# Pooled attention with a feed-forward layer: one block maximum as the bias of the exponential, half-height transposes, a ring of three banks for the maxima

## The chip, the cores and the metric

One core of one Trainium2 chip. The metric is the device time of one execution in microseconds: the median of the timed runs. TensorE is called PE, VectorE DVE, ScalarE ACT, GpSimd POOL, SyncE SP.

## The reference

Inputs q, k, v are 4 x 8 heads x 1152 x 64 in float32, drawn with a deviation of about 0.71 (0.1 x 7.123 and 0.1 x 7.13) for q and k. Queries are averaged two by two, so there are 576 per head.

```python
q_pool = q.reshape(B, H, S // 2, 2, D).mean(axis=3)
scores = 1.0 / np.sqrt(D) * np.matmul(q_pool, k.transpose(0, 1, 3, 2))
scores = scores - np.max(scores, axis=-1, keepdims=True)
attn = np.exp(scores)
attn = attn / (np.sum(attn, axis=-1, keepdims=True) + 1e-09)
attn_out = np.matmul(attn, v)                                  # (4, 8, 576, 64)
x = attn_out.transpose(0, 2, 1, 3).reshape(4 * 576, 512)
h = np.maximum(x @ w_in, 0.0)                                  # 512 -> 2048
out = (h * h) @ w_out                                          # 2048 -> 512
```

## The kernel before

`run` builds the whole computation twice: once with quick maxima, and once more (`exact`) behind a flag that is read at the end (a branch on `again`); with these inputs the second isn't executed. In it stand first the attention, then the feed-forward part.

**Attention.** Work goes by pairs of heads, 16 of them (`pairs`, index n). The two heads of a pair lie on partitions 0 to 63 and 64 to 127, so a matmul of one head uses half of the array's rows and the two heads' matmuls stand side by side (`rows(h)`). For a pair: `load_q`, `load_k`, `load_v` (DMAs from SP); `pool_q` adds neighbouring queries on POOL; `prep` (units u = 0 to 3) transposes keys and queries on PE into a PSUM bank; `prep_high` (ACT) writes the rounded high part and `prep_low` (DVE) the remainder, so that a product is made from three matmuls. `squares` (ACT) keeps sums for the flag.

`maxes` (12 units) computes quick scores with queries on the partitions, in two PSUM banks, one for each head; `max_left` reduces them on DVE to a negated maximum for each query row, `max_fin` joins the parts, `max_turn` transposes the result on PE and `max_rows` copies it on ACT into `MM`, a row of negated maxima for each query.

The queries are then taken in two halves (e = 0, 1) of 288. `scores` makes for each of 9 chunks of 128 keys a tile of keys x queries of both heads: four terms of two matmuls, the three products and a matmul of ones with `MM`, which subtracts each query's maximum. `expo` (ACT) writes the exponential into a buffer `p` (three buffers in all, each for a run of 4 or 5 chunks, `CYCLE`). `pv` multiplies with the values on PE (stationary values of 64 columns for each head, so the array is used in another shape). `add` sums the exponentials of the nine chunks on POOL with four instructions in a half (L375); `total` sums over the partitions on PE; `total_x` (ACT) copies, `recip` (DVE) inverts in two pieces, `pv_x` (ACT) brings out the values' result and `scale_x` (POOL, L398) multiplies.

**PSUM.** 8 banks: score tiles 2 x 2 banks (`sps`), maxima 2 (`mps`, one tile for both heads), 1 for transposes and totals (`tps`, handed out by `bank`), 1 for values (`vps`).

**The order** is written out by hand: `at(key, name, fn, ..., after=...)` gives each step a key, raised to just behind the keys of the steps named in `after`; all steps are sorted by key and issued in that order, and each engine works through its own steps in that order. The numbers in `AT` shift the steps' keys. A pair has 4 units of key (`NCY`); pair n's scores start at key 4 n.

In the last pair (n = 15) the weights of the feed-forward part are converted on DVE between the other steps (`convert`, key -0.8 to 3.4 after the pair's start; L111 to L125, POOL joins with L127).

**Feed-forward.** Five passes over 5 blocks of tokens; `layer1` and `layer2` with three matmuls for each product; `out_rows` gives for a tile of 128 tokens the rows of the output and `layer2` sends them, alternating between the queues of SP and ACT.

Of the kernel before, what the change touches and what calls it, by code (L numbers as in the profile page):

```python
# [21 lines left out]
    e=-0.666, h0=-1.798, h1=-0.099, h2=0.09, h3=-0.731, l0=-2.259, l1=-1.892, l2=-1.181, l3=-2.391, m0=3.23,  # L22
    mr0=-0.125, mr1=0.928, pq=-0.619, px=1.044, r0=-0.773, r1=-3.214, r10=-0.653, r11=-2.477, r2=0.853, r3=0.12,
    r4=-1.46, r5=-1.28, r6=-0.268, r7=-0.491, r8=-0.663, r9=-0.675, rc00=0.606, rc01=0.974, rc10=-2.759,
    rc11=-1.537, sq0=2.106, sq1=-0.737, sq2=2.477, sx=-0.655, t0=1.92, t1=2.58, tx=0.115, u0=-3.77, u1=0.23,
    u2=0.55, u3=1.23, x0=1.22, x1=1.3, x10=4.46, x11=2.14, x2=-1.95, x3=2.22, x4=2.46, x5=1.53, x6=3.05, x7=3.22,
    x8=3.53, x9=4.14,
# [3 lines left out]
EXACT = 8192.0  # L31


@with_exitstack
def kernel(
# [31 lines left out]
    def run(ctx, exact):  # L67
# [89 lines left out]
        with ExitStack() as a:  # L157
# [6 lines left out]
            mps = a.enter_context(tc.tile_pool(name="mps", bufs=1, space=PSUM))  # L164
            tps = a.enter_context(tc.tile_pool(name="tps", bufs=1, space=PSUM))
# [5 lines left out]
            QQ = [[kq.tile([P, NQ], F32R, name=f"qq{i}{m}") for m in range(2)] for i in range(2)]  # L171
# [5 lines left out]
            NM = [kq.tile([P, 2, 64], F32, name=f"nm{i}") for i in range(2)]  # L177
            MM = [[kq.tile([P, NH], F32R, name=f"mm{i}{m}") for m in range(2)] for i in range(2)]
            MASK = kq.tile([P, NT5], F32, name="mask")
            ONER = kq.tile([P, P], F32R, name="oner")  # L180
# [4 lines left out]
            SQ = kq.tile([P, 3, NP], F32, name="sq")  # L185
            ld_, qp_, b_, s_, m_, p_, t_, pv_, r_ = ({} for _ in range(9))
# [24 lines left out]
            def pool_q(n):  # L211
                qt, ql = ld_.pop(("q", n))
                qp = ld.tile([P, NR, 2, D], F32, tag="qp", name="qp")
                qpl = ld.tile([NL, 2, D], F32, tag="qpl", name="qpl")
                nc.gpsimd.tensor_tensor(out=qp.rearrange("p r h d -> p h r d"), in0=qt[:, :, :, 0, :],
                                        in1=qt[:, :, :, 1, :], op=ALU.add)
                nc.gpsimd.tensor_tensor(out=qpl, in0=ql[:, :, 0, :], in1=ql[:, :, 1, :], op=ALU.add)
                qp_[n] = qp, qpl


            def squares(n, e):
                x = [ld_["k", n], *qp_[n]][e]
# [272 lines left out]
            for x in NM:  # L495
                nc.vector.memset(x, 0.0)
# [161 lines left out]
```

## Time and profile before

| | |
|---|---|
| timed runs | 916.15, 916.32, 917.96 us; median 916.32 |
| profiled execution, span from first to last instruction | 914.7 us |
| busy: PE / DVE / POOL / ACT | 874.5 / 651.7 / 481.0 / 449.4 us |
| score matmuls (L332), the three products | 1728 |
| score matmuls (L332), with ones | 576 |
| maxima L303, reductions of 128 x 1024 | 160 |
| output DMAs | 28 (8 of 256 KB, 20 of 128 KB) |

The profile holds one execution. Its own time outside the span isn't recorded; the median of the timed runs lies 1.6 us above the span. Engines run beside each other; a long busy time is no bound by itself, and matmuls are pipelined, so that their shown durations overlap. Durations of one instruction are means in ns where a group is shown, and the start and length in us where single instructions are shown.

### The profile page before, as it was taken

Reading aid. Unit: us, or ns where it says so; the run is one execution under the profiler, and the core shown is the slowest. Engines: PE = TensorE matmul, PEld = TensorE weight load, DVE = VectorE, ACT = ScalarE, POOL = GpSimd, SP = SyncE. Lnnn points to the kernel's source line nnn. Section 1 sums busy time; section 2 is a strip of 40 time slices with the busy share of each in tenths; the row PEclk is TensorE's granted clock in tenths of the full one; section 3 lists DMA queues with packets and bytes.
Section 4 is the critical chain, followed back from the end, with each engine's and each line's share of the span. In section 5 each row is a group of like instructions: output and inputs, shape, how many; then the busy total and the mean of one; then the engine's idle time right before and its main releaser. Section 6 shows DMA issues by size and latency. Waiting matters only on the chain.

```text
span 914.7 us, 15275 instructions
## 1 busy us (share of the span) xinstructions
PE 874.5 (96%) x6182; PEld 649.2 (71%) x6182; DVE 651.7 (71%) x849; ACT 449.4 (49%) x876; POOL 481.0 (53%) x261
## 2 busy tenths in 40 slices
PE   6999999999999999999968989999999999999996
PEld 4666666666666666666635868778888888888885
DVE  5667667676776767776799998988877676655543
ACT  2665665666656566665625546333342433333321
POOL 1488988898888988889786342431320311110000
PEclk9999999999999999999979999999999999999999
DMA  7122222122221222230011121211210101000213
GB/s 206 27 64 65 56 73 59 56 60 70 54 78 52 54 78 53 79 98 2 27 47 47 47 70 47 69 51 42 59 51 30 47 24 47 24 1 1 70 47 95
DMA packets 61968, 50.88 MB, mean 56 GB/s; under 512 B 39104, under 2 KB 49344, under 8 KB 61888
## 3 DMA queue, kind: packets, MB, share of 16 engines
q1 hardware_dynamic: 61088, 48.50, 18.5%
q10 hardware_dynamic: 800, 1.31, 0.4%
q8 instruction: 50, 0.82, 0.4%
q14 instruction: 30, 0.25, 0.1%
HBM read 45.09 MB, written 4.72 MB: 54 GB/s over the span
## 4 chain that ended last, share of the span: by engine, by line
PE 79%; DVE 11%; issue 3%; ACT 3%; POOL 2%; DMA 1%; SPq 0%; ACTq 0%; DVEq 0%; POOLq 0%
PE o L580 17%; PE h L543 17%; PE s L332 16%; PE pv L349 16%; PE m L291 7%; DVE pm L303 4%; PE t L243 2%; PE t L385 2%; POOL r L127 1%; DVE a L116 1%; DVE xlo L150 1%; ACT p L342 1%; PE t L249 1%; DVE h L119 1%; PE t L314 1%
## 5 line engine op out<-in xcount | busy, mean ns | idle before, releaser
L303 DVE TENSOR_REDUCE pm<-m 128x2 f32<-128x1024 f32 x154 | 188.5, 1224 | 58.1 <-PE m L291 58.0
L342 ACT ACTIVATE p<-s 128x576 f32<-128x576 f32 x288 | 176.9, 650 | 67.6 <-PE s L332 63.3
L375 POOL TENSOR_TENSOR ts<-p 128x2304 f32<-128x2304 f32 (+1 forms) x32 | 157.4, 4918 | 58.8 <-ACT p L342 58.8
L332 PE MATMUL s<-qq,kk 64*128 64x288 f32 x1728 | 174.5, 311 | 1.9 <-ACT p L342 1.2
L543 PE MATMUL h<-xhi,wi 128*128 128x512 f32 (+1 forms) x600 | 171.1, 370 | 3.4 <-ACT wi L137 3.4
L580 PE MATMUL o<-wo,gh 128*128 128x512 f32 x540 | 167.3, 391 | 2.5 <-DVE part L588 2.4
L349 PE MATMUL pv<-p,vt 128*64 128x288 f32 x1152 | 158.5, 416 | 0.0
L127 POOL TENSOR_TENSOR r<-r,h 128x512 f32<-128x512 f32 x32 | 51.4, 1607 | 202.3 <-DVE r L125 193.3
L332 PEld LDWEIGHTS s<-qq,kk 64*128 64x128 f32 x1728 | 129.5, 186 | 34.2 <-issue 19.6
L543 PEld LDWEIGHTS h<-xhi,wi 128*128 128x128 f32 x600 | 110.6, 190 | 23.7 <-ACT wi L137 3.6
L375 POOL TENSOR_TENSOR ts<-ts 128x1152 f32<-128x1152 f32 (+1 forms) x60 | 121.6, 2027 | 4.7
L349 PEld LDWEIGHTS pv<-p,vt 128*64 128x64 f32 x1152 | 78.0, 138 | 60.2 <-issue 16.3
L580 PEld LDWEIGHTS o<-wo,gh 128*128 128x128 f32 x540 | 100.1, 188 | 24.8 <-DVE part L588 2.2
L543 PE MATMUL h<-xlo,wi 128*128 128x512 f32 (+1 forms) x300 | 110.7, 369 | 0.0
L580 PE MATMUL o<-wo,gl 128*128 128x512 f32 x270 | 105.2, 389 | 0.0
L550 ACT CAST gh<-g 128x512 fp32r<-128x512 f32 (+1 forms) x80 | 46.4, 579 | 115.8 <-DVE g L547 58.5
L291 PE MATMUL m<-kk,qq 64*128 64x512 f32 (+1 forms) x468 | 86.5, 400 | 11.0 <-DVE pm L303 9.1
L551 DVE TENSOR_TENSOR gl<-g,gh 128x512 fp32r<-128x512 f32 (+1 forms) x80 | 57.0, 713 | 41.9 <-ACT gh L550 41.6
L332 PE MATMUL s<-mm,oner 64*128 64x288 f32 x576 | 85.4, 292 | 0.0
L150 DVE TENSOR_TENSOR xlo<-xt,xhi 128x1024 fp32r<-128x1024 f32 (+7 forms) x40 | 59.9, 1496 | 25.8 <-ACT xhi L149 25.7
L547 DVE SCALAR_TENSOR_TENSOR g<-h,r 128x512 f32<-128x512 f32 (+1 forms) x80 | 50.6, 633 | 36.9 <-ACT r L545 36.8
L291 PEld LDWEIGHTS m<-kk,qq 64*128 64x128 f32 x468 | 41.2, 189 | 42.7 <-DVE pm L303 17.7
(101 smaller groups left out, 1091.2 us busy)
## 6 DMA issues: line engine op xcount, KB each, us to landing
kt<-in_k_dram SPq DMA_DIRECT2D x32, 288.0 KB, 4.3
vt<-in_v_dram SPq DMA_DIRECT2D x16, 576.0 KB, 3.9
qt<-in_q_dram SPq DMA_DIRECT2D x16, 512.0 KB, 3.9
raw<-in_moe_w_in_dram SPq DMA_DIRECT2D x16, 512.0 KB, 3.8
raw<-in_moe_w_out_dram SPq DMA_DIRECT2D x16, 512.0 KB, 3.4
out_dram<-part SPq DMA_DIRECT2D x8, 256.0 KB, 2.5
out_dram<-part SPq DMA_DIRECT2D x10, 128.0 KB, 2.6
out_dram<-part ACTq DMA_DIRECT2D x10, 128.0 KB, 3.4
```

The source lines that it names most:

```text
L127: nc.gpsimd.tensor_tensor(out=r, in0=r, in1=h.bitcast(F32), op=ALU.add)
L150: nc.vector.tensor_tensor(out=l, in0=x, in1=h, op=ALU.subtract)
L291: nc.tensor.matmul(out=m[:, h, o], lhsT=l[rows(h), TQ[t]:TQ[t] + P], rhs=r[rows(h), ks], start=(x == 0), stop=(x == len(terms) - 1))
L303: nc.vector.tensor_reduce(out=pm[:, :, ts, g], in_=m, op=ALU.max, axis=AX.X, negate=True)
L332: nc.tensor.matmul(out=s[:, h, :NH], lhsT=l[rows(h)], rhs=r[rows(h)], start=(i == 0), stop=(i == 3))
L342: nc.scalar.activation(out=p_[n, e, r][:, i], in_=s_.pop((n, e, c))[:, :, :NH], func=ACTF.Exp)
L349: nc.tensor.matmul(out=pv_[n, e][rows(h), :NH], lhsT=ld_["v", n][:, h, c, :], rhs=p_[n, e, r][:, i, h, :], start=(c == 0), stop=(c == NC - 1))
L375: nc.gpsimd.tensor_tensor(out=t[:, o], in0=part(x or 0), in1=part(y), op=ALU.add)
L543: nc.tensor.matmul(out=h, lhsT=w, rhs=x, start=(m == 0), stop=(m == len(mm) - 1))
L547: nc.vector.scalar_tensor_tensor(out=g, in0=h, scalar=0.0, in1=r, op0=ALU.max, op1=ALU.mult)
L551: nc.vector.tensor_tensor(out=gl, in0=g, in1=gh, op=ALU.subtract)
L580: nc.tensor.matmul(out=acc[i][t], lhsT=g, rhs=w, start=(first and m == 0), stop=(last and m == 2))
```

## The change

- Scores: the fourth term (ones times `MM`) goes. `max_fin` now reduces all maxima of a half, of both heads, to one column `PB`; `max_turn` transposes this column spread over 128 columns; `max_rows` reduces the result on DVE to one value for each partition, the same on all, `NB_`, the block's negated maximum; `expo` takes it as its bias. So `expo`, not `scores`, comes after `max_rows`.
- A flag more: `scale_x` takes on DVE the largest reciprocal of a half (`RM`); at the end these are compared with `SPREAD`, and the flag is set if one is above.
- `total_x` adds 1e-30 and scales by 1 + 1e-9 instead of adding 1e-9.
- Transposes: `turn` makes two of 64 rows instead of one of 128; their results lie in the two banks of a score tile. `bank` now hands out score tiles; the pool `tps` is gone. Queries come out in another order (`QQ` is 640 wide, the left-over queries are padded to 128 rows with zeros in `QL`), and `out_rows` maps pieces of 64 rows back.
- Maxima: one bank for each head, from a ring of three; a `max_left` is two reductions, one for each head.
- All numbers of `AT`; `CYCLE` stays (4, 5), so the values of a half are taken in two runs, four in a pair. The last two pairs (`late`) don't shift the totals' steps. In the first pair the highs and lows have keys of their own.

The diff, cut (new values of `AT` in full; `exact` branches and the rewriting of `parts` left out):

```diff
 AT = dict(
+    e=-7.93, h0=-10.461, h1=-8.334, h2=-12.648, h3=0.439, l0=-18.883, l1=-11.573, l2=-2.152, l3=-16.38, m0=4.007,
+    mr0=-7.093, mr1=-30.302, pq=-1.536, px=-9.71, r0=-22.81, r1=-4.332, r10=-5.139, r11=-9.398, r2=-8.51, r3=-10.162,
+    r4=-22.014, r5=-11.202, r6=-9.322, r7=-17.694, r8=-1.801, r9=-15.75, rc00=-22.507, rc01=-10.607, rc10=-16.061,
+    rc11=-42.226, sq0=-0.054, sq1=1.971, sq2=2.567, sx=2.904, t0=2.581, t1=2.595, tx=-9.192, u0=-0.554, u1=0.507,
+    u2=-0.413, u3=1.422, x0=3.434, x1=0.095, x10=5.199, x11=-9.348, x2=0.215, x3=2.21, x4=2.45, x5=1.407, x6=3.335,
+    x7=3.133, x8=4.734, x9=4.371,
...
+SPREAD = 4096.0
...
-            mps = a.enter_context(tc.tile_pool(name="mps", bufs=1, space=PSUM))
-            tps = a.enter_context(tc.tile_pool(name="tps", bufs=1, space=PSUM))
+            mps = a.enter_context(tc.tile_pool(name="mps", bufs=3, space=PSUM))
...
+            QL = kq.tile([P, 2, D], F32, name="ql")
+            PB = [kq.tile([P, 2], F32, name=f"pb{i}") for i in range(2)]
+            NB_ = [kq.tile([P, 2], F32, name=f"nb{i}") for i in range(2)]
...
+            RM = kq.tile([P, 2 * NP], F32, name="rm")
...
-            def bank(n=1):
-                if n:
-                    return tps.tile([P, 512], F32, tag="t", name="t")
-                return sps.tile([P, 2, 512], F32, tag="s", name="s")[:, 0]
-
-
+            def bank():
+                return sps.tile([P, 2, 512], F32, tag="s", name="s")
+
+            def turn(x, t):
+                for z in range(2):
+                    nc.tensor.transpose(out=t[:, z], in_=x[rows(z)], identity=ident[rows(z), rows(z)])
+
+            def halves(x):
+                return x.rearrange("p z (i k) -> p i z k", k=64)
...
                 for i in cs:
-                    nc.tensor.transpose(out=t[:, o:o + P], in_=kt[:, i].rearrange("p h d -> p (h d)"), identity=ident)
-                    o += P
+                    turn(kt[:, i].rearrange("p h d -> p (h d)"), t[:, :, o:o + 64])
+                    o += 64
...
                     m = sps.tile([P, 2, 512], F32, tag="s", name="s")
+                    m = [m[:, h] for h in range(2)]
                 else:
-                    m = mps.tile([P, 2, 512], F32, tag="m", name="m")
+                    m = [mps.tile([P, 512], F32, tag="m", name="m") for _ in range(2)]
...
-                if g == 2:
-                    nc.vector.tensor_reduce(out=pm[:, :, ts[0]:ts[-1] + 1, 2],
-                                            in_=m[:, :, :len(ts) * P].rearrange("p h (t k) -> p h t k", k=P),
-                                            op=ALU.max, axis=AX.X, negate=True)
-                else:
-                    nc.vector.tensor_reduce(out=pm[:, :, ts, g], in_=m, op=ALU.max, axis=AX.X, negate=True)
+                for h in range(2):
+                    if g == 2:
+                        nc.vector.tensor_reduce(out=pm[:, h, ts[0]:ts[-1] + 1, 2],
+                                                in_=m[h][:, :len(ts) * P].rearrange("p (t k) -> p t k", k=P),
+                                                op=ALU.max, axis=AX.X, negate=True)
+                    else:
+                        nc.vector.tensor_reduce(out=pm[:, h, ts, g:g + 1], in_=m[h], op=ALU.max, axis=AX.X, negate=True)
 
             def max_fin(n, e):
+                if not exact:
+                    nc.vector.tensor_reduce(out=PB[n % 2][:, e:e + 1], in_=PM[n % 2][:, :, 2 * e:2 * e + 3], op=ALU.min, axis=AX.XYZ)
+                    return
                 t = slice(3 * e, 3 + 2 * e)
...
-                t = bank(n or e)[:, :P] if t is None else t
-                nc.tensor.transpose(out=t, in_=NM[n % 2].rearrange("p h t -> p (h t)"), identity=ident)
+                t = bank()[:, :, :64] if t is None else t
+                turn(NM[n % 2].rearrange("p h t -> p (h t)") if exact else PB[n % 2][:, e:e + 1].broadcast_to([P, P]), t)
                 b_[n, "m", e] = t
 
             def max_rows(n, e):
                 t = b_.pop((n, "m", e))
+                if not exact:
+                    nc.vector.tensor_reduce(out=NB_[n % 2][:, e:e + 1], in_=t, op=ALU.min, axis=AX.XY)
+                    return
...
-                for i, (l, r) in enumerate(((kh[:, ks], qh[:, qs]), (kl[:, ks], qh[:, qs]), (kh[:, ks], ql[:, qs]),
-                                            (ONER, MM[n % 2][e]))):
+                terms = [(kh[:, ks], qh[:, qs]), (kl[:, ks], qh[:, qs]), (kh[:, ks], ql[:, qs])]
+                if exact:
+                    terms.append((ONER, MM[n % 2][e]))
+                for i, (l, r) in enumerate(terms):
                     for h in range(2):
-                        nc.tensor.matmul(out=s[:, h, :NH], lhsT=l[rows(h)], rhs=r[rows(h)], start=(i == 0), stop=(i == 3))
+                        nc.tensor.matmul(out=s[:, h, :NH], lhsT=l[rows(h)], rhs=r[rows(h)], start=(i == 0), stop=(i == len(terms) - 1))
...
-                nc.scalar.activation(out=p_[n, e, r][:, i], in_=s_.pop((n, e, c))[:, :, :NH], func=ACTF.Exp)
+                nc.scalar.activation(out=p_[n, e, r][:, i], in_=s_.pop((n, e, c))[:, :, :NH], func=ACTF.Exp,
+                                     bias=0.0 if exact else NB_[n % 2][:, e:e + 1])
...
+                    nc.vector.tensor_reduce(out=RM[:, 2 * n + e:2 * n + e + 1], in_=r_[n, e], op=ALU.max, axis=AX.X)
                 nc.gpsimd.tensor_tensor(out=x, in0=x, in1=r_.pop((n, e)), op=ALU.mult)
...
-                        at(cy + .1 + .08 * i, ("s", n, e, c), scores, n, e, c, after=[("mr", n, e)] + [("lo", n, u) for u in range(4)])
-                        at(cy + .16 + .08 * i + A["e"], ("e", n, e, c), expo, n, e, c, after=[("s", n, e, c)])
+                        at(cy + .1 + .08 * i, ("s", n, e, c), scores, n, e, c, after=([("mr", n, e)] if exact else []) + [("lo", n, u) for u in range(4)])
+                        at(cy + .16 + .08 * i + A["e"], ("e", n, e, c), expo, n, e, c, after=[("s", n, e, c), ("mr", n, e)])
...
+                    late = n < NP - 2
                     if (n, e) == (NP - 1, 1):
                         t = base + NCY + .9
                     at(t, ("tot", n, e), total, n, e, after=[("add", n, e, na - 1)])
-                    at(t + A["tx"], ("tx", n, e), total_x, n, e, after=[("tot", n, e)])
+                    at(t + A["tx"] * late, ("tx", n, e), total_x, n, e, after=[("tot", n, e)])
                     for i in range(2):
-                        at(t + A[f"rc{e}{i}"], ("rc", n, e, i), recip, n, e, i, after=[("tx", n, e)])
-                    at(t + A["sx"], ("sx", n, e), scale_x, n, e, after=[("rc", n, e, 0), ("rc", n, e, 1), ("px", n, e)])
+                        at(t + A[f"rc{e}{i}"] * late, ("rc", n, e, i), recip, n, e, i, after=[("tx", n, e)])
+                    at(t + A["sx"] * late, ("sx", n, e), scale_x, n, e, after=[("rc", n, e, 0), ("rc", n, e, 1), ("px", n, e)])
...
+                y = kq.tile([P, 4], F32, name="y")
+                nc.vector.tensor_reduce(out=y[:, 0:3], in_=SQ, op=ALU.max, axis=AX.X)
+                nc.vector.tensor_reduce(out=y[:, 3:4], in_=RM, op=ALU.max, axis=AX.X)
+                nc.vector.tensor_scalar(out=y[:, 3:4], in0=y[:, 3:4], scalar1=SPREAD, scalar2=None, op0=ALU.is_gt)
+                t = bank()[0:1, 0]
+                nc.tensor.matmul(out=t[:, 0:4], lhsT=ONE[:, 0:1], rhs=y, start=True, stop=True)
...
+                y = out[b * NQ:b * NQ + NR * P].rearrange("(p r) d -> r p d", r=NR)
+                g, p0 = divmod(o, 64)
+                r, z = ((g % (NR - 1), g // (NR - 1)) if g < 2 * (NR - 1) else (NR - 1 + g % 2, (g - 2 * (NR - 1)) // 2))
+                m = min(n, 64 - p0)
+                p0 += 64 * z
+                yield c - t * P, m, y[r, p0:p0 + m] if r < NR else out[b * NQ + NR * P + p0:b * NQ + NR * P + p0 + m]
```

## Rows read from the trace of the kernel before

**Rows 1.** Page, whole span: busy us, share, instructions of PE

```profile
PE 874.5 (96%) x6182; PEld 649.2 (71%) x6182; DVE 651.7 (71%) x849; ACT 449.4 (49%) x876; POOL 481.0 (53%) x261
```

**Rows 2.** Stretches: us, busy of PE, PEld, DVE, ACT, POOL, granted clock, DMA

```profile
35.97:438.56 402.59, 399.83 (x3776) 269.01 (x3776) 277.88 (x320) 253.07 (x546) 340.42 (x167) 1.00 0.23 63
...
208.16:236.95 28.79, 28.58 (x270) 19.19 (x270) 19.99 (x23) 18.12 (x40) 24.37 (x13) 1.00 0.23 63
...
452.24:498.52 46.28, 36.41 (x313) 23.03 (x309) 44.69 (x39) 17.37 (x33) 37.10 (x22) 0.89 0.15 46
```

**Rows 3.** Timeline, POOL, one pair: start, us, instructions [idle before <-releaser]

```profile
208.16 5.12 POOL L375 TENSOR_TENSOR ts<-p 128x2304 f32<-128x2304 f32 x1 [2.48 <-ACT p L342]
...
218.94 0.80 POOL L398 TENSOR_TENSOR xt<-xt,r 128x288 f32<-128x288 f32 x1
...
221.70 5.12 POOL L375 TENSOR_TENSOR ts<-p 128x2304 f32<-128x2304 f32 x1 [0.31 <-ACT p L342]
...
228.40 4.12 POOL L375 TENSOR_TENSOR ts<-ts 128x1152 f32<-128x1152 f32 x2
...
233.66 0.80 POOL L398 TENSOR_TENSOR xt<-xt,r 128x288 f32<-128x288 f32 x1 [1.14 <-DVE nm L307]
...
236.95 5.10 POOL L375 TENSOR_TENSOR ts<-p 128x2304 f32<-128x2304 f32 x1 [2.49 <-ACT p L342]
```

**Rows 4.** Chain of waits, same pair: start, us, what

```profile
206.90 1.24 DVE pm L303
...
211.82 0.66 ACT p L342
```

**Rows 5.** Timeline, PE, same pair

```profile
206.69 0.56 PE L332 MATMUL s<-qq,kk 64*128 64x288 f32 x6
207.09 0.30 PE L332 MATMUL s<-mm,oner 64*128 64x288 f32 x2
207.24 0.66 PE L332 MATMUL s<-qq,kk 64*128 64x288 f32 x6
...
220.84 0.66 PE L243 MATMUL t<-ident,kt 128*128 128x128 f32 x4
...
221.43 0.66 PE L332 MATMUL s<-qq,kk 64*128 64x288 f32 x6
...
234.01 0.27 PE L252 MATMUL t<-ident,qpl 64*128 64x64 f32 x1
234.22 0.33 PE L314 MATMUL t<-ident,nm 128*128 128x128 f32 x1
```

**Rows 6.** Groups by line, 36 to 439 us: busy, mean ns | idle before

```profile
L303 DVE TENSOR_REDUCE pm<-m 128x2 f32<-128x1024 f32 x140 | 171.4, 1224 | 53.5 <-PE m L291 53.5
...
L394 DVE RECIPROCAL r<-r 128x144 f32<-128x144 f32 x54 | 54.7, 1033 | 0.0
...
L267 DVE TENSOR_TENSOR kk<-t,kk 128x512 fp32r<-128x512 f32 x28 | 19.4, 692 | 46.1 <-ACT kk L262 46.1
...
L299 DVE TENSOR_REDUCE pm<-m 128x6 f32<-128x768 f32 x14 | 13.4, 958 | 7.4 <-PE m L291 7.4
...
L299 DVE TENSOR_REDUCE pm<-m 128x4 f32<-128x512 f32 x14 | 9.7, 694 | 17.2 <-PE m L291 17.2
...
L307 DVE TENSOR_REDUCE nm<-pm 128x6 f32<-128x18 f32 x14 | 2.4, 173 | 0.5
```

**Rows 7.** Timeline, DVE in a middle pair, DVE and PE in the last pair

```profile
229.78 1.04 DVE L394 RECIPROCAL r<-r 128x144 f32<-128x144 f32 x1
...
453.88 3.74 DVE L116 TENSOR_SCALAR a<-a 128x512 int32<-128x512 int32 x1
...
465.19 0.80 PE L291 MATMUL m<-kk,qq 64*128 64x512 f32 x2 [6.88 <-DVE pm L303]
465.91 5.04 PE L349 MATMUL pv<-p,vt 128*64 128x288 f32 x20
...
481.50 2.60 PE L349 MATMUL pv<-p,vt 128*64 128x288 f32 x20
```

More of the change, by code (lines that the diff above doesn't have):

```diff
@@ L290, in maxes @@
                         for h in range(2):
-                            nc.tensor.matmul(out=m[:, h, o], lhsT=l[rows(h), TQ[t]:TQ[t] + P], rhs=r[rows(h), ks],
+                            nc.tensor.matmul(out=m[h][:, o], lhsT=l[rows(h), TQ[t]:TQ[t] + P], rhs=r[rows(h), ks],
                                              start=(x == 0), stop=(x == len(terms) - 1))
@@ L377, in total @@
             def total(n, e):
-                t = bank()
+                t = bank()[:, 0]
                 xs = [t_[n, e][:, 0]]
@@ L397, in scale_x @@
                 x = x_part(n, e)
+                if not exact:
+                    nc.vector.tensor_reduce(out=RM[:, 2 * n + e:2 * n + e + 1], in_=r_[n, e], op=ALU.max, axis=AX.X)
                 nc.gpsimd.tensor_tensor(out=x, in0=x, in1=r_.pop((n, e)), op=ALU.mult)
@@ L489, in run @@
                 at(last + 2.7 + u, ("w", u), split_w, u, cv, "wf", 2, after=[("cv", u, NCV - 1)])
-            nc.vector.tensor_tensor(out=MASK, in0=ident[:, 0:NT5], in1=ident[:, 64:64 + NT5], op=ALU.add)
-            nc.vector.memset(ONER.bitcast(F32), 1.0)
+            if exact:
+                nc.vector.tensor_tensor(out=MASK, in0=ident[:, 0:NT5], in1=ident[:, 64:64 + NT5], op=ALU.add)
+                nc.vector.memset(ONER.bitcast(F32), 1.0)
+                for x in NM:
+                    nc.vector.memset(x, 0.0)
             nc.vector.memset(ONE, 1.0)
             nc.vector.memset(SQ, 0.0)
-            for x in NM:
-                nc.vector.memset(x, 0.0)
+            nc.vector.memset(QL, 0.0)
             warm = kq.tile([1, 1], F32, name="warm")
@@ L499, in run @@
             nc.scalar.activation(out=warm, in_=warm, func=ACTF.Exp)
-            t = bank()
+            t = bank()[:, 0]
             for i in range(WARM):
@@ L512, in run @@
             if not exact:
-                y = kq.tile([P, 3], F32, name="y")
-                nc.vector.tensor_reduce(out=y, in_=SQ, op=ALU.max, axis=AX.X)
-                t = bank()[0:1]
-                nc.tensor.matmul(out=t[:, 0:3], lhsT=ONE[:, 0:1], rhs=y, start=True, stop=True)
+                y = kq.tile([P, 4], F32, name="y")
[4 more added lines that the diff above has]
+                nc.tensor.matmul(out=t[:, 0:4], lhsT=ONE[:, 0:1], rhs=y, start=True, stop=True)
                 z = kq.tile([1, 4], F32, name="z")
-                nc.vector.tensor_copy(out=z[:, 0:3], in_=t[:, 0:3])
+                nc.vector.tensor_copy(out=z, in_=t[:, 0:4])
                 nc.vector.tensor_tensor(out=z[:, 1:2], in0=z[:, 1:2], in1=z[:, 2:3], op=ALU.add)
                 nc.vector.tensor_tensor(out=z[:, 0:1], in0=z[:, 0:1], in1=z[:, 1:2], op=ALU.mult)
-                nc.vector.tensor_scalar(out=z[:, 3:4], in0=z[:, 0:1], scalar1=(EXACT / QS) ** 2, scalar2=None, op0=ALU.is_gt)
-                nc.vector.tensor_copy(out=flag, in_=z[:, 3:4])
+                nc.vector.tensor_scalar(out=z[:, 0:1], in0=z[:, 0:1], scalar1=(EXACT / QS) ** 2, scalar2=None, op0=ALU.is_gt)
+                nc.vector.tensor_tensor(out=z[:, 0:1], in0=z[:, 0:1], in1=z[:, 3:4], op=ALU.max)
+                nc.vector.tensor_scalar(out=z[:, 0:1], in0=z[:, 0:1], scalar1=1.0, scalar2=None, op0=ALU.min)
+                nc.vector.tensor_copy(out=flag, in_=z[:, 0:1])
         wp = ctx.enter_context(tc.tile_pool(name="wp", bufs=WB))
```

70 lines of the change are left out of this document (31 added, 39 removed).

## Prediction

> **What bounds the kernel now.** I read the page first. TensorE (PE) is busy 96% of the span [rows 1]. The table of stretches splits this: from 36 to 439 us PE is busy 399.8 of 402.6 us, at full clock; POOL 340.4, VectorE (DVE) 277.9, ScalarE (ACT) 253.1 [rows 2]. That stretch holds 14 periods, one for each pair of heads: the long POOL addition comes back every 402.6 / 14 = 28.76 us [rows 2, 3]. The third view, the chain of waits, shows the same pieces each period: nearly all on PE, apart from one wait for a maximum on DVE (1.24 us) and one for an exponential on ACT (0.66 us) [rows 4]. With some 0.2 us of issue around these, PE itself needs 28.8 - 1.24 - 0.66 - 0.2 = 26.7 us for a pair; its busy share is higher because matmuls overlap and are shown longer than their spacing. So inside the attention PE sets the pace.
>
> The stretch 452 to 498 us, the last pair, is another regime: DVE is busy 44.7 of 46.3 us, PE 36.4 [rows 2]. From 498.5 us to the end at 914.7 runs the feed-forward part; the change leaves its loops alone.
>
> **The score passes (PE).** Scores lose the fourth of four accumulating matmuls. Two heads run side by side. In a tile in mid-stream the first three terms start 0.40 us before the ones matmuls (206.69 to 207.09), and these 0.15 us before the next tile (207.24) [rows 5]. So a term costs 0.40 / 3 = 0.13 us at least and 0.15 at most; I take 0.13, three terms against one. 18 tiles in a pair x 0.13 = 2.34 us (up to 2.7).
>
> **Transposes and order (PE).** Four transposes now take 0.59 us (220.84 to 221.43) [rows 5]; 16 of them in a pair make 2.4 us. Each becomes two of 64 rows, side by side in two banks, in the array shape that scores and maxima already use. No row shows two half transposes together. If they overlap, two of them cost what a score term costs, 16 x 0.13 = 2.1 us: 0.3 saved. If they don't, the nearest row is the one transpose of 64 rows (64 columns), which takes 0.21 us to the next instruction (234.01 to 234.22) [rows 5] with a change of array shape in it; two of them at most 0.4, 6.7 us: 4.3 lost. I take the first, since scores of the same shape overlap, and keep 1 us of loss in the range. The values' matmuls stand in five groups and the totals by themselves twice; sorting the new keys gives four groups with each total right in front of one. The transposes' own five visits to another shape end as well. I put 0.1 us on each of the some six visits saved (an estimate: 0.21 us for the lone transpose less 0.13 for a term): 0.6 us. PE after: 26.7 - 2.34 - 0.3 - 0.6 = 23.5 us; with 1 us lost on transposes 24.8, with all 4.3 lost 28.1.
>
> **DVE.** It is busy 20.0 us in a pair [rows 2]. Added: (a) the maximum of a unit is two instructions of 512 columns. 768 columns take 958 ns and 512 take 694, so 1.03 ns a column and 0.16 us fixed [rows 6]. 12 more instructions x 0.16 = 2.0 us, or some 1.0 us if back-to-back instructions overlap by half of their fixed part. (b) `max_rows` moves from ACT to DVE: 128 PSUM columns, 0.16 + 0.13 = 0.3 us x 2. (c) `scale_x` gets a maximum over 288 columns for the flag, 0.16 + 0.30 = 0.46 us x 2, bounded by 0.17 us (18 columns) and 0.69 us (512) [rows 6]. (d) Small: `max_fin` has the same input as before, the last lows are 256 wide instead of 192 (0.07 us). Sum 20.0 + (2.6 to 3.6) = 22.6 to 23.6 us.
>
> **ACT** loses the copies of `max_rows` and stays far below its limit: 18.1 us busy now [rows 2].
>
> **POOL.** The change takes nothing from it. In the period shown it waits 2.48, 0.31 and 1.14 us, so its work and the small gaps in it take 28.79 - 3.93 = 24.86 us [rows 3]. This is the new floor: no pair can be faster than 24.9 us. All three engines then lie close, PE 23.5, DVE 23, POOL 24.9.
>
> **Does the order let POOL run full?** Keys are sorted and each engine works in that order. POOL's scaling of half 1 of pair 5 gets key 26.595 + 2.904 = 29.499, just ahead of the additions of pair 7 (29.5): it is two pairs late and waits for nothing. Now POOL waits there 1.14 us [rows 3]. The first long addition of a half waits for its eighth exponential. The exponentials 5 to 9 of a half need a buffer that the long addition of the half before frees; POOL then still has 5.7 us of short additions to do (208.16 + 5.12 to 218.94) [rows 3], against four exponentials of 0.66 us [rows 4]. That is slack of 3 us. On the other side, all uses of the former transpose bank now go through the two score tiles: four preparations, one maximum and two totals next to 18 scores. Queued behind: a preparation holds a tile until ACT and then DVE have read it (DVE's low alone 0.69 us [rows 6]), and the scores wait. The worst place is the end of a pair: preparations 0 and 2 of the next pair, then `max_turn` behind `max_fin`, behind both lows on DVE. Four chunks of values (2.1 us) stand between as cover; without it PE would idle 1 to 1.5 us. The exponentials, no longer the scores, wait for the maximum, so PE runs two tiles ahead. The ring of three banks lets one head's maximum start while the other is read, which removes the 1.24 us wait [rows 4]. I add 0.35 us to POOL's floor for what does not fit: 25.2 us a pair. Bounds: 24.9, and 26.5 if the shared score tiles cost what the ring gains.
>
> **Ends.** Lead-in to 36 us: eight first score tiles lose 8 x 0.13 = 1 us of passes, the nine first maxima gain 9 x 0.16 = 1.5 us, waits as that of 1.24 us [rows 4] go: -1 (between -2 and +1.5). Half of pair 14 before the last pair: -1.2. The last pair is bound by DVE, whose SBUF operations there last until a POOL addition ends (3.74 us for L116) [rows 7]. DVE gets about 4 us more work there (five split maxima, two `max_rows`, up to seven flag maxima), and by the keys `max_fin` of pair 15 now stands behind four more conversion steps (59.987 against 59.21; cv 0.4 is at 59.9), so exponentials of pair 15 wait for them. Before, PE waited there on the maxima anyway until 465 us [rows 7]. I take +4, from 0 to +7. The flag's matmul now waits for the last reciprocal and two small reductions: +0.5. Output rows leave as 36 DMAs of 64 rows rather than 28; they overlap the last matmuls but for the last ones: 0, at most 1 us.
>
> **Sum.** 14 x (28.76 - 25.2) = 49.8; -49.8 - 1 - 1.2 + 4 + 0.5 = -47.5 us. The profiled span is 914.7 us, the median of the timed runs 916.3, so 1.6 us lie around it. 914.7 - 47.5 + 1.6 = 868.8, say 869.
>
> **Rivals.**
> A, PE stays the bound. The scores shrink, but the half transposes cost an us and the shared score tiles put the waits back, or two such losses together: 28.76 - 2.34 = 26.4 us a pair. -33 - 1.2 + 4.5 = -30, or 886. For it: two tiles for 25 uses. Against it: three banks, and four array changes fewer.
> B, DVE becomes the bound. 23.6 us plus the 3 us that it must wait for in-order neighbours (now it idles 8.8 us a pair, half of that for PE's maxima) gives 26.6 us: 888.
> C, slower: the new flag maximum reads SBUF while POOL adds. If it were held as L116 is (3.74 us) [rows 7], two of them would cost DVE up to 2 x 5.1 us a pair, the length of POOL's long addition [rows 3]. DVE would need 23.1 + 10 = 33 us and the kernel 14 x 4.4 + 10 = 70 us more, 985. It decides from 2.8 us of delay for each (23.1 + 5.7 = 28.8). Against it: the reciprocals work in SBUF with one operand, as the new maximum does; one took 1.04 us at 229.78, in the middle of POOL's addition from 228.40 to 232.5, and the mean of 54 is 1033 ns [rows 3, 6, 7]; the maxima L307 read SBUF too and average 173 ns. The Trainium skill, page "SBUF — State Buffer", section "Who interferes with whom", says that VectorE and GpSimd contend for one port pair, held for a whole instruction, and that `tensor_reduce` on trn2 never takes part. By that rule this rival is out; the trace agrees as far as 18 columns go.
> D, the clock falls. Once PE is not the bound it idles about 1.3 us a pair in bits. After its 6.9 us wait in the last pair the twenty value matmuls took 5.04 us against 2.60 later [rows 7]: the lower level, half. If a quarter of PE's work ran so, 23.5 x 1.25 = 29.4 us a pair, slower than now: 14 x 0.6 + 3 = 11 us, 928. Against it: PE now waits 2.1 us a pair and the granted clock is 1.00 throughout [rows 2, 4]. The Trainium skill, "TensorE: Matmul & The Clock Gate", section "A second HAM failure mode: psum-queue depth-cycling", tells of a kernel that cycles through PSUM banks, idles briefly between groups and oscillates between the clock levels, which speaks against a ring of banks. No stretch of this trace shows it.
> E, the change doesn't do what it says: a block maximum far above a row's own maximum sets the new flag, and the whole kernel runs again. By the reference's inputs a score has a deviation of 0.71 x 0.5 x 8 / 8 = 0.36; For a row's sum over 1152 keys to fall under 1/4096, the block's maximum would have to lie ln(1152 x 4096) = 15.4 above the row's mean, 43 deviations. It can't.
>
> **Chances.** Forecast 0.74 (own range 861 to 878), A 0.12, B 0.09, C 0.015, D 0.015, no change 0.02. The range takes in A and B: 860 to 889. About 0.2% is what a measurement of this kernel can tell from no change. Faster by more than that 0.95, within it 0.02, slower 0.03.
>
> **What would show it.** Period of POOL's long additions 25.2 us, POOL with under 1 us of waiting in a pair; 18 score tiles of three terms, 0.40 us apart; maxima of 0.69 us each; flag maxima near 0.46 us; PE's waits moved to ACT's exponentials; the last pair 46 to 52 us. A period over 26 us, or POOL waiting over 1.5 us in it, makes the step on the shared score tiles wrong. Flag maxima over 1 us mean rival C.

## The result and the profile after

The changed kernel takes 892.8 us (median of four runs, 890.1 to 894.1) against 916.2 us of the kernel before in the same rounds: ratio 0.973, 95% interval 0.971 to 0.976. Forecast were 869 us and a range of 860 to 889: the sign was right, but the gain of 23.4 us is half of the 47.5 forecast, and the time lies outside the range. The profiled run, the fastest of the four, took 890.05 us, 887.9 us of it span.

Engines over the whole span of the kernel after (page, first part):

```profile
PE 826.3 (93%) x5862; PEld 615.3 (69%) x5862; DVE 679.6 (77%) x1106; ACT 452.4 (51%) x780; POOL 476.8 (54%) x261
```

PE lost 48 us of work against [rows 1], 320 matmuls fewer (576 with ones are gone, 256 half transposes came). The span lost 26.8. The stretches that answer to [rows 2] (us, busy time of PE, PEld, DVE, ACT, POOL, granted clock, DMA):

```profile
34.95:411.51 376.56, 359.28 (x3498) 237.78 (x3498) 305.48 (x542) 255.46 (x461) 337.74 (x167) 1.00 0.25 65
209.07:236.01 26.94, 25.71 (x250) 17.05 (x250) 22.03 (x40) 18.28 (x34) 24.23 (x13) 1.00 0.26 68
424.19:473.00 48.81, 33.80 (x264) 21.29 (x262) 44.87 (x53) 18.09 (x29) 38.27 (x24) 0.86 0.14 44
```

The first is the fourteen pairs: 376.56 / 14 = 26.90 us for one, where 25.2 were forecast. The 1.7 us over it make 23.8 us in fourteen pairs. That is more than the whole miss of the profiled span (887.9 us against 914.7 - 47.5 = 867.2, 20.7 us); the ends together came out 3 us better than forecast. The POOL timeline of one pair, as [rows 3]:

```profile
209.07 5.10 POOL L397 TENSOR_TENSOR ts<-p 128x2304 f32<-128x2304 f32 x1
222.86 5.10 POOL L397 TENSOR_TENSOR ts<-p 128x2304 f32<-128x2304 f32 x1 [2.24 <-ACT p L363]
236.01 5.10 POOL L397 TENSOR_TENSOR ts<-p 128x2304 f32<-128x2304 f32 x1
```

POOL waits once in a pair, for the eighth exponential: 26.94 - 2.24 = 24.7 us of work and small gaps. The period stays above the forecast floor of 24.9, since POOL has to wait. The chain of waits from 200 to 260 us says what is late (shares by engine and line, then pieces as start, us, what):

```profile
by line: PE pv L371 34.2%; PE s L353 28.5%; ACT p L363 18.3%; PE m L301 8.6%; PE s L407 5.9%; PE s L237 3.7%; issue 2.1%; ACTq L363 0.1%
...
207.03 0.74 ACT p L363
207.77 0.74 ACT p L363
...
208.53 0.75 ACT p L363
...
214.43 1.38 ACT p L363 x2
...
215.86 0.71 PE s L407 x4
```

In the same view of the kernel before, exponentials hold 2.2% of the chain, one piece of 0.66 us in a pair [rows 4]. Now they hold 18.3%, 4.9 us of 26.94: the chain passes through ACT wherever PE needs one of the two score tiles that an exponential still reads, also in front of a total (215.86). PE isn't idle in all of this time, since it can be filling the other tile; the 4.9 us are ACT's share of the path.

Groups by line, whole span (busy us, mean ns | idle before):

```profile
L363 ACT ACTIVATE p<-s,nb 128x576 f32<-128x576 f32 x288 | 201.6, 739 | 81.0 <-PE s L353 63.9
L314 DVE TENSOR_REDUCE pm<-m 128x1 f32<-128x512 f32 x308 | 195.8, 685 | 48.0 <-PE m L301 46.2
L422 DVE TENSOR_REDUCE rm<-r 128x1 f32<-128x288 f32 x32 | 14.2, 444 | 0.1
L334 DVE TENSOR_REDUCE nb<-s 128x1 f32<-128x128 f32 x32 | 9.2, 287 | 8.1 <-PE s L237 8.1
```

DVE's new work has the forecast sizes (0.69, 0.46 and 0.3 us). The exponential, whose change of price the prediction left out, went from 650 to 739 ns.

### The profile page after: what moved, and what is told of

Its sections match the earlier page's. It is cut to its first block, busy times and chain, and to the rows that moved or that the text cites. A ratio compares the mean times of both kernels' runs of the same rounds, so it can differ in the third digit from the quotient of the medians.

```text
span 887.9 us, 14808 instructions
## 1 busy us (share of the span) xinstructions
PE 826.3 (93%) x5862; PEld 615.3 (69%) x5862; DVE 679.6 (77%) x1106; ACT 452.4 (51%) x780; POOL 476.8 (54%) x261
## 4 chain that ended last, share of the span: by engine, by line
PE 75%; DVE 11%; ACT 9%; issue 3%; DMA 1%; POOL 1%; SPq 0%; ACTq 0%; DVEq 0%; POOLq 0%
PE o L611 20%; PE h L575 19%; PE pv L371 15%; PE s L353 13%; ACT p L363 8%; PE m L301 4%; PE s L407 2%; PE s L237 2%; DVE pm L314 2%; DVE h L120 1%; DVE xlo L151 1%; DVE a L117 1%; DVE a L114 1%; DVE r L417 1%; DVE a L124 1%
## 5 line engine op out<-in xcount | busy, mean ns | idle before, releaser
L363 ACT ACTIVATE p<-s,nb 128x576 f32<-128x576 f32 x288 | 201.6, 739 | 81.0 <-PE s L353 63.9
L314 DVE TENSOR_REDUCE pm<-m 128x1 f32<-128x512 f32 x308 | 195.8, 685 | 48.0 <-PE m L301 46.2
L128 POOL TENSOR_TENSOR r<-r,h 128x512 f32<-128x512 f32 x32 | 47.3, 1477 | 204.3 <-DVE r L126 190.4
L371 PE MATMUL pv<-p,vt 128*64 128x288 f32 x1152 | 153.6, 411 | 0.0
L371 PEld LDWEIGHTS pv<-p,vt 128*64 128x64 f32 x1152 | 84.6, 137 | 49.2 <-issue 1.4
L577 ACT ACTIVATE r<-h 128x512 f32<-128x512 f32 (+1 forms) x80 | 44.3, 554 | 60.1 <-PE h L575 55.1
L575 PEld LDWEIGHTS h<-xlo,wi 128*128 128x128 f32 x300 | 56.5, 188 | 9.3
```

Source lines behind the costliest of these rows:

```text
L128: nc.gpsimd.tensor_tensor(out=r, in0=r, in1=h.bitcast(F32), op=ALU.add)
L314: nc.vector.tensor_reduce(out=pm[:, h, ts, g:g + 1], in_=m[h], op=ALU.max, axis=AX.X, negate=True)
L363: nc.scalar.activation(out=p_[n, e, r][:, i], in_=s_.pop((n, e, c))[:, :, :NH], func=ACTF.Exp, bias=0.0 if exact else NB_[n % 2][:, e:e + 1])
L371: nc.tensor.matmul(out=pv_[n, e][rows(h), :NH], lhsT=ld_["v", n][:, h, c, :], rhs=p_[n, e, r][:, i, h, :], start=(c == 0), stop=(c == NC - 1))
L575: nc.tensor.matmul(out=h, lhsT=w, rhs=x, start=(m == 0), stop=(m == len(mm) - 1))
```

## Experiments

All are single runs unless a ratio is given, and four runs of the changed kernel lie 4 us apart. Periods are steadier. Each is the time in which POOL's long additions go through the fourteen pairs, divided by 14; in three kernels whose pairs were expected to take the same time (the changed one, x2 and x14) it is 26.90, 26.92 and 26.90 us. Two theories were on the table: that the bias operand makes the exponentials too slow (T in the first expectations), and that the shared score tiles hold PE (S there). The last runs, x19 and x20, name theirs anew, with other letters.

**The bias operand.** First the operand is taken away, then it is given a constant column, so that no exponential waits for a maximum.

```diff
-  nc.scalar.activation(out=..., func=ACTF.Exp, bias=0.0 if exact else NB_[n % 2][:, e:e + 1])
+  nc.scalar.activation(out=..., func=ACTF.Exp)             # x1_no_bias
+  nc.scalar.activation(out=..., func=ACTF.Exp, bias=CB)    # x2_const_bias, CB a column of -2
```

> The changed kernel with the exponential's bias operand left out (softmax needs no maximum for these inputs); maxima, transposes and max_rows still run and nobody reads their result. Theory T (price of the bias operand): an exponential falls from 739 ns back to about 650 and four in a row from 2.88 to about 2.3 us, PE's waits on exponentials shrink, the period of POOL's long additions falls from 26.9 to 25.0 to 25.4 us, the span by 20 to 27 us to about 863. Theory S (the two score tiles shared by 25 uses cost it): period stays at 26.5 to 26.9, span 882 to 888.

> The changed kernel with a constant column (-2) in place of the block maximum as bias: the operand stays, the wait for max_rows goes. Theory T: exponentials 739 ns as before, period 26.6 to 26.9, span 883 to 888. If it is the wait for the maximum that costs (theory W): period 25.0 to 25.8, span 863 to 873.

Without the operand: 877.8 us, period (397.73 - 33.81) / 14 = 25.99. With a constant one: 893.4 us, 26.92, as the changed kernel. So it is the operand itself and not the wait for the maximum behind it, and it is worth 0.9 us a pair, 12.4 us of span (887.9 to 875.5): half of the 1.7 us a pair and no more. The rows of exponentials on ACT in the changed kernel:

```profile
212.93 2.88 ACT L363 ACTIVATE p<-s,nb 128x576 f32<-128x576 f32 x4 [1.29 <-PE s L353]
...
219.91 3.75 ACT L363 ACTIVATE p<-s,nb 128x576 f32<-128x576 f32 x5 [0.47 <-POOL ts L397]
```

and without the operand:

```profile
212.67 1.20 ACT L363 ACTIVATE p<-s 128x576 f32<-128x576 f32 x2 [0.49 <-PE s L353]
214.08 1.20 ACT L363 ACTIVATE p<-s 128x576 f32<-128x576 f32 x2 [0.21 <-PE s L353]
215.48 0.65 ACT L363 ACTIVATE p<-s 128x576 f32<-128x576 f32 x1 [0.20 <-PE s L353]
```

A row of five lasts 3.75 us with it and 3.46 without (212.67 to 216.13). Without it they come in twos, with a wait for scores of 0.2 us after each two: still (3.46 - 0.65) / 4 = 0.70 us a tile, where three terms cost PE 0.40. In this kernel exponentials hold 16.0% of the chain, 4.2 us a pair.

The same operand in the kernel before, where PE had no wait for ACT to speak of:

> The kernel before, all four terms, with a constant zero column as bias operand of the exponential. Theory T (an operand costs about 0.09 us and the overlap with the next exponential): exponentials 739 ns and 0.72 to 0.75 us apart instead of 0.55; since ACT has slack there and PE is the bound, the period rises only from 28.8 to 29.0 to 29.6, span 917 to 927. If the operand costs nothing by itself: 650 ns and 914 to 916.

923.3 us, period 28.92 against 28.76; the exponentials take 744 ns. The operand costs 0.2 us a pair there and 0.9 in the changed kernel: the edit's price depends on what PE has lost before.

**The fourth term by itself**, put back into the changed kernel (`terms.append((ONER, MM[n % 2][e]) if exact else (ONEZ, MZ))`, ones against zeros), and taken out of the kernel before:

> The changed kernel with a fourth score term put back (ones times zeros, read from constant tiles); the bias stays. Theory T: PE waits for ACT during the exponentials, so of 18 x 0.13 = 2.3 us a pair only a part shows: period 27.5 to 28.3, span 896 to 907. If PE sets the pace everywhere (rival A of the prediction): period 29.2, span 920.

> The kernel before with only the fourth score term left out (no maximum is subtracted; all else, the maxima and max_rows too, still runs in the old order). PE set the pace there, so the whole 2.3 us of a pair should show if nothing else is late: period 26.4, span 879 to 883 (theory T, the price of the operand isn't paid). If the order or POOL holds it: period 27.2 to 28, span 892 to 903.

Put back: 909.3 us, (428.64 - 35.30) / 14 = 28.10, so 1.2 us a pair of the 2.34. Pieces of the chain say why it is half, in the changed kernel and then with the fourth term:

```profile
205.52 0.75 ACT p L363
206.27 0.04 issue
206.31 0.69 PE s L353 x6
207.00 0.02 issue
207.03 0.74 ACT p L363
```

```profile
221.26 0.75 ACT p L364
222.01 0.04 issue
222.06 0.81 PE s L354 x8
222.87 0.02 issue
```

Here PE begins to write a score tile again when the exponential that reads it has ended; three terms then take 0.69 us until the next exponential begins. With the hand-overs (0.04 and 0.02 us, "issue") the loop takes 0.75 + 0.04 + 0.69 + 0.02 = 1.50 us. Both tiles go through it side by side, so it brings two tiles, one in 0.75 us. With the fourth term the loop is 1.62, so 0.06 us a tile more, where the term takes 0.13 of PE's time: over 18 tiles an estimate of 1.1 us, and 1.2 were measured. Without the operand the loop has 0.66 in place of 0.75 (x1, chain at 224.78); half of the difference over 18 tiles is 0.8 us (an estimate as well), and 0.9 were measured.

Taken out of the kernel before alone: 906.3 us, 27.94, so 0.8 us. Its chain of waits, 200 to 260 us:

```profile
by line: PE pv L348 31.8%; PE s L331 16.7%; PE m L291 16.2%; DVE pm L303 10.3%; ACT p L341 4.3%; PE t L384 4.2%; DVE pm L299 3.2%; PE t L243 3.0%; PE t L249 2.4%; DVE kk L267 2.3%; PE t L314 2.2%; ACT kk L262 1.8%; issue 1.1%; PE t L252 1.0
```

Maxima on DVE (L303 and L299) have 13.5% where they had 4.1%, 3.8 us a pair for 1.2: in the old order, with one tile of two banks for the maxima, waits for them take back most of what the passes save. What the ring of three is worth by itself this run doesn't show, since it keeps the old order and the whole transposes too; in the changed kernel no maximum on DVE is left in the chain.

**A bank for the totals, taken from the ring:**

```diff
-            mps = a.enter_context(tc.tile_pool(name="mps", bufs=3, space=PSUM))
+            mps = a.enter_context(tc.tile_pool(name="mps", bufs=2, space=PSUM))
+            tps = a.enter_context(tc.tile_pool(name="tps", bufs=1, space=PSUM))
...
-                t = bank()[:, 0]
+                t = tps.tile([P, 512], F32, tag="t", name="t")
```

> The changed kernel with a bank of its own for the totals, taken from the ring of maxima (two instead of three). Theory S (PE waits where a total needs a score tile that ACT still reads): those waits of about 0.7 us in each half go, period 25.6 to 26.5, unless two banks for the maxima give it back. If the ring's third bank is what matters: period 27.5 to 28.5 with waits on DVE maxima.

899.2 us, 27.34. Its chain, same stretch:

```profile
by line: PE pv L372 32.5%; PE s L354 24.5%; PE m L302 15.3%; DVE pm L315 8.6%; ACT p L364 7.1%; PE t L408 5.3%; PE s L238 4.9%; issue 1.0%; DVE nb L335 1.0%; ACTq L364 0.1%
```

The exponentials' share falls from 18.3 to 7.1%, and maxima on DVE, which had none, take 8.6%. Both of the prediction's halves show here: totals in the score tiles cost time, the third bank gains some, and the eight banks don't hold both (4 + 3 + 1 + 1 = 9).

**Totals later.** Moving the totals behind the values should free the score tiles where exponentials stand in a row (`t0=2.73, t1=2.73`).

> The changed kernel with the totals issued behind the five value matmuls instead of ahead of them (t0 and t1 at 2.73), all else as it is, the bias operand too. Theory S: PE goes straight from the fourth score tile to the values while ACT empties the score tiles, period 25.8 to 26.4, span 872 to 881. Theory T alone (ACT's own pace of 0.72 us for each exponential is the chain): period 26.6 to 26.9, span 884 to 888.

990.0 us, and neither theory's forecast came. `sx` counts from the total, so POOL's scaling moved behind the additions of the next half; ACT's copy of the total waits for the buffer that it frees, and DVE's reciprocals for the copy. POOL's additions have 51% of the chain. Without the bias operand it took the same, 990.0. With `sx=2.755` the scaling stays where it was:

> The changed kernel, bias kept, totals behind the five value matmuls, and POOL's scaling at its old key (sx 2.755), so that it stays ahead of the additions. Theory S (PE waits where a total needs a score tile that ACT still reads, 1.4 us in a pair): period 25.4 to 25.8, span 866 to 872. Theory T alone (ACT's pace of 0.72 us an exponential): period 26.6 to 26.9.

942.8 us, and 925.7 without the operand: now the reciprocals, put right behind the total, stand in front of DVE's maxima (DVE r L417 13.1% of the chain). With keys for the reciprocals as well (`rc00=rc01=0.25, rc10=rc11=0.45`):

> Totals behind the values once more, the bias operand kept, and now the reciprocals behind one pair of maxima on DVE (rc00 and rc01 0.25, rc10 and rc11 0.45), so that DVE no longer stands in front of the maxima until ACT has copied the total. Theory S (score tiles that totals need hold PE, 1.4 us a pair): period 25.3 to 25.9. Theory T alone (ACT's pace): 26.6 to 26.9. If DVE's order still binds: above 27 with waits of PE on maxima.

918.9 us, period 28.42, as the last branch of the expectation has it; 915.9 us without the operand. Pieces of the chain:

```profile
202.80 1.87 DVE r L417 x2
206.34 2.09 PE pv L371 x16
...
215.62 1.28 DVE pm L314 x2
216.90 1.87 DVE r L417 x2
218.77 0.87 DVE pm L310 x2
219.64 1.04 DVE pm L314 x2
```

Exponentials are down to 2.5% of the chain, and DVE's reciprocals and maxima have 30%. This family doesn't tell how much the tiles cost, since each shift changed another engine's order. It shows that none of the three orders tried is as good as that of the changed kernel, where DVE has 22 us of work in 27.

**No maxima at all.** In the quick part the maxima and the bias are left out; the flag takes the largest and the smallest reciprocal, the three banks go to a third score tile (two banks) and the totals stand behind the values (`t0=2.73, t1=2.73, sx=2.755`). x21 is x15 again, x19 has two tiles in place of three, x20 three tiles and the operand.

> Quick maxima and their bias left out altogether in the first, quick part; the flag watches the sums' reciprocals at both ends instead. Three score tiles in place of two (the maxima's banks are free), totals behind the values. PE loses 3 us a pair, DVE 17. If POOL's 24.86 us of work are the floor, as the prediction said, the period is 24.9 to 25.1 in spite of that, span 852 to 862; if PE's and DVE's share still matters, it would be below 24.8, which the floor excludes.

> The kernel without the quick part's maxima and bias again (three score tiles, nothing changed), timed against the kernel before in three rounds, for an interval. One look gave 856.5 us. Expected 854 to 860 us, ratio 0.932 to 0.938.

> The kernel without the quick part's maxima and without the bias (the one with three score tiles, period 25.02 us, POOL nearly full), with one size changed: two tiles for scores, preparations and totals instead of three, as the changed kernel has. DVE has little to do here and the exponentials are the short ones of 650 ns, so nothing else stands in PE's way. Theory T (two shared tiles make PE and ACT take turns): the period rises to 25.7 to 26.2 us, the exponentials take 10% or more of the chain of waits, 866 to 874 us. Theory S (what the kernel without bias had over POOL's floor came from DVE's maxima): the period stays at 25.0 to 25.2 us, 856 to 859 us.

> The same kernel with three score tiles, with one operand added: each exponential of the quick part takes a constant column (-2) as bias. Theory T (the longer, no longer overlapping exponentials cost only because PE has to wait for one of two tiles): with a third tile they are covered, period 25.0 to 25.3 us, 856 to 861 us, ACT busy some 1.6 us a pair more than without the operand. Theory U (the operand costs on ACT itself, whatever the tiles): 18 exponentials, 0.15 to 0.2 us further apart where they stand in a row, period 25.8 us or more, 868 us or more.

Three tiles: 857.2 us in three rounds, ratio 0.933, interval 0.931 to 0.936; period 25.02. Two tiles (`bufs=2`): 851.6 us, period (373.17 - 28.18) / 14 = 24.64. Three tiles with the operand: 856.9 us, 25.04. POOL's timeline with two tiles, the ends of the fourteen pairs:

```profile
28.18 5.11 POOL L401 TENSOR_TENSOR ts<-p 128x2304 f32<-128x2304 f32 x1 [10.44 <-ACT p L368]
...
373.17 5.10 POOL L401 TENSOR_TENSOR ts<-p 128x2304 f32<-128x2304 f32 x1
```

From 100 to 370 us POOL waits for nothing: its work is the bound, 24.6 us a pair. So two shared tiles alone don't hold the period at 26; I had expected 25.7 to 26.2 of them. The other sign of that theory did come, exponentials with over 10% of the chain of waits from 200 to 260 us:

```profile
by line: PE pv L375 38.9%; PE s L358 29.1%; ACT p L368 20.9%; PE s L238 4.6%; PE s L411 4.0%; issue 2.8%; ACTq L368 0.3%
```

That is 5.1 us a pair, and no piece on POOL. PE and ACT take turns here as in the changed kernel, and without the maxima their path has shrunk to about the length of POOL's work. In the first pairs, from 52 to 126 us, the runs of sixteen value matmuls come 24.57 to 24.60 us apart by pairs, just ahead of POOL's 24.67; the loop alone would hardly go faster than POOL.

With a third tile the operand costs nothing in the period. But POOL is nearly full in both kernels with three tiles (3.8 and 3.4 us of waits from 100 to 370 us), which hides a price as well, so ACT's rows have to tell (first without, then with the operand):

```profile
214.84 2.28 ACT L368 ACTIVATE p<-s 128x576 f32<-128x576 f32 x4 [0.94 <-PE s L358]
220.30 2.82 ACT L368 ACTIVATE p<-s 128x576 f32<-128x576 f32 x5 [0.18 <-PE s L358]
```

```profile
217.67 2.64 ACT L369 ACTIVATE p<-s,cb 128x576 f32<-128x576 f32 x4 [2.28 <-PE s L359]
...
223.32 3.27 ACT L369 ACTIVATE p<-s,cb 128x576 f32<-128x576 f32 x5 [0.18 <-POOL ts L402]
```

| a row of five exponentials | us | a tile |
|---|---|---|
| three tiles, no operand | 2.82 | (2.82 - 0.65) / 4 = 0.54 |
| three tiles, operand | 3.27 | 0.63 |
| two tiles, no operand | 3.46 | 0.70 |
| two tiles, operand (the changed kernel) | 3.75 | 0.75 |

The first two are ACT's own pace; neighbours overlap by 0.11 us with the operand and without. With two tiles, ACT, PE's three terms and the hand-over follow one another in the loop shown above, and half of each ns by which an exponential grows stands in a tile's time. (The kernels with three tiles have no maxima between the scores, so the table compares rows and not whole pairs.)

Loading and converting the feed-forward weights one pair earlier (`last - 8` for `last - 4`, `last - 4.8` for `last - .8`), to relieve the last pair:

> The version without quick maxima (period 25.0 us) with the weight conversions begun one pair earlier, where DVE has 17 us of room in a pair, instead of in the last pair, which DVE bound for 46 to 50 us. POOL keeps its 24.86 us a pair; its conversions (4 x 1.5 us) move with them. The last pair then takes 30 to 38 us: time 838 to 850 us. If the conversions hold POOL by the port that both read, the period of pair 14 grows by 5 us or more and the gain is under 5 us: 850 to 858.

865.2 us, ratio 0.944, interval 0.942 to 0.946, against 857.2 with 0.933, so slower and not the 838 to 850 expected: DVE's conversions then stand before the preparation of the last pairs (PE waits up to 8.5 us for `qq`, and the last three long additions come 20 us apart).

**The ends.** In the changed kernel, the last pair's `m0` back to 3.23, and the flag without its reciprocal part:

```diff
-                t = pre + A["m0"] if n else -20
+                t = pre + (A["m0"] if n < NP - 1 else 3.23) if n else -20
```

> The changed kernel with two edits to its end alone: the last pair's first maximum is finished ahead of the weight conversion (its key 3.23 in place of 4.007), and the final flag no longer reads the largest reciprocals, so that its matmul waits for nothing late. Theory: PE's wait of 8.1 us for the last pair's maximum goes or moves, and the 3.7 us before the flag's matmul go; the stretch from POOL's last long addition to the first layer-1 matmuls of converted weights gets 3 to 7 us shorter, span 881 to 885. If DVE is saturated there, the first edit gives nothing and only 2 to 4 us of the second show. Period 26.95.

889.0 us, 1.0 us under the lowest run of the changed kernel and so no clear gain; the span of 886.8 lies above the 881 to 885 expected. The turn of pair 15 comes 3.8 us earlier, but later waits give it back. PE in the last pair, the changed kernel, then this run:

```profile
434.58 0.37 PE L237 MATMUL s<-ident,pb 64*128 64x64 f32 x2 [8.12 <-DVE pb L318]
...
448.93 0.27 PE L237 MATMUL s<-ident,pb 64*128 64x64 f32 x2 [2.30 <-DVE pb L318]
...
473.89 0.19 PE L547 MATMUL s<-y,one 128*1 128x4 f32 x2 [3.67 <-DVE y L545]
```

```profile
430.83 0.37 PE L237 MATMUL s<-ident,pb 64*128 64x64 f32 x2 [6.67 <-DVE pb L318]
444.98 0.49 PE L301 MATMUL m<-kk,qq 64*128 64x512 f32 x1 [1.65 <-DVE pm L314]
449.16 0.37 PE L237 MATMUL s<-ident,pb 64*128 64x64 f32 x2 [1.38 <-DVE pb L318]
```

## Why the prediction missed

**Bound before, passes, DVE, POOL: right in kind.** PE set the pace before. DVE's new instructions cost what was said; it is busy 22.0 us a pair, a little under 22.6 to 23.6. The half transposes came out by the cheap one of the two cases: in the chain eight of them take 0.46 us to the values behind them (209.33 to 209.79), where four whole ones took 0.59 [rows 5]. The ring did away with the waits on maxima, which have no piece in the chain. POOL's floor was 24.64 us in the run with two tiles and no maxima, 0.2 under the 24.9 that no pair was to beat. Rival B is out, though its 888 us lie near: DVE is busy 22.0 of 26.9 us and has no piece in the chain from 200 to 260 us. Rival C is out: the flag maximum took 444 ns in the mean of 32, 454 at most, while POOL was busy 24.2 of 26.9 us. The Trainium skill, "SBUF — State Buffer", "Who interferes with whom", says that `tensor_reduce` never contends on trn2; the trace agrees. Rival D is out for this kernel: the granted clock of the fourteen pairs is 1.00. Rival E is out: the page counts 1728 score matmuls as before, so nothing ran a second time.

**The step that failed** is the one on ACT, "stays far below its limit: 18.1 us busy now", and with it "I add 0.35 us to POOL's floor for what does not fit". By the prediction's own sign (a period over 26 us, POOL waiting over 1.5) it is the step on the shared score tiles, which comes to the same: the tiles are held by exponentials. The prediction does say that PE's waits would move to the exponentials. It looked at ACT's share, not at its pace in a row, and so gave all that doesn't fit 0.35 us. Before, a tile's four terms took PE 0.55 us [rows 5], and exponentials came in twos, 0.54 apart. ACT's rows of one half, in the kernel before:

```profile
218.54 1.19 ACT L342 ACTIVATE p<-s 128x576 f32<-128x576 f32 x2 [0.72 <-PE s L332]
...
220.43 1.19 ACT L342 ACTIVATE p<-s 128x576 f32<-128x576 f32 x2
...
222.27 0.65 ACT L342 ACTIVATE p<-s 128x576 f32<-128x576 f32 x1
```

Rows of four and five tiles stood there too, but with four terms a tile, and maxima and transposes between the tiles, this row of five took 4.4 us (218.54 to 222.92), and PE set its pace. In the changed order a tile has three terms, 0.40 us, and no transposes stand inside a row. PE gets ahead of ACT there, and the loop over two tiles sets 0.70 us a tile, or 0.75 with the longer exponentials. Inside the rows the missing fourth term therefore pays by half: 1.2 of 2.34 us show (x3). In the chain this is 4.9 us on exponentials a pair, next to 21.4 on PE and 0.6 of issue, where the sum had 23.5 on PE and let POOL's 24.9 and 0.35 stand above it. (The 21.4 aren't all of PE's work: what it does under an exponential isn't in the chain.)

What is shown of the 1.7 us a pair: 0.9 is the operand. It had no term at all, though its price was to be had. The Trainium skill, "ScalarE: Activation LUTs", "What ACT_TABLE_LOAD costs", gives about 93 ns for each pointer operand; the trace gives 739 - 650 = 89. The other 0.8 (25.99 to 25.2) goes with the path through PE and ACT: without the operand exponentials still hold 4.2 us of it, and when the maxima's 10.9% (2.8 us a pair) are gone, POOL's floor is reached with the same two tiles. That is argued and not shown by itself, since x19 moves the totals too. How much a third tile would gain with the maxima in place stays open: it would leave them one bank, and no run tries it. Nor was the operand tried with two tiles and no maxima. Rival A came nearest, with PE staying on the path at 26.4 us a pair: the shared score tiles do put waits back, as it says, but the half transposes cost nothing, and the operand isn't in it.

**Ends.** Lead-in: first long addition at 34.95 against 35.97, -1.0 as forecast. Half of pair 14 (411.51 to 424.19): 12.7 us against 13.7, -1.0 against -1.2. From the last long addition (424.19) to the first matmul with the weights `wi` in the feed-forward: 54.6 us against 48.9, +5.7 where 4 + 0.5 were forecast; the place was right (PE waits 8.12 us for `max_fin` behind conversions) and DVE is full there, 44.9 of 48.8 us. The rest of the feed-forward took 409.1 us against 413.5, -4.4, which I had not forecast and can't explain by a run. Sum: -1.0 - 26.0 - 1.0 + 5.7 - 4.4 = -26.7, the span's difference.

**Flag.** Its matmul waits 3.67 us for the reciprocal maximum, where 0.5 was forecast. x14 leaves that away, and the feed-forward's first matmul comes 2.4 us earlier, counted from the last long addition; x14 has the edit of `m0` in it too, so this isn't the flag's alone.

## What to carry to other kernels

Where one engine gets faster, look up at what pace the next one takes its output in a row, not how busy it is over the span: with two buffers, one pass of the loop (both engines' work on a buffer and the hand-over) brings two of them, and a ns saved on either engine counts by half. An operand that changes from a constant to a column belongs into the sum; here 18 times 89 ns a pair were 1.6 us on ACT, and 0.9 showed. Try a deletion before a rebalancing: leaving the maxima out, with a flag for rows that leave the range, gave 851.6 us (one run, with the totals moved) where their cheaper form gave 892.8.

## What was not expected of the hardware

The kernel without maxima was slower with a third score tile, 857.2 us (855.7 to 857.9 in four runs) against 851.6 in one run, and its clock was lower. PE in one pair with three tiles (x15):

```profile
236.31 0.59 PE L238 MATMUL s<-ident,qp 64*128 64x64 f32 x6 [3.37 <-POOL qp L220]
236.83 4.11 PE L375 MATMUL pv<-p,vt 128*64 128x288 f32 x16
```

PE ran ahead of POOL, waited 3.37 us for the queries, and the sixteen value matmuls after it took 4.11 us against 2.16 elsewhere in the same kernel: the lower of the two levels, 1.2 of 2.4 GHz. From 30 to 370 us the granted clock was 0.91 with three tiles and 1.00 with two. The pairs take 25.02 and 24.64 us, and 14 x 0.38 = 5.3 us is most of the 5.6 between the two kernels. Whether the clock or the order makes it, no run tells apart.
